# A fourth staging place for late operands, and filter groups of 1024 columns instead of 864, in an H3 convolution woven into a feed-forward network

## The chip, the cores and the metric

The kernel runs on one core of one Trainium2 chip. The metric is the device time of one execution in microseconds (us). A core has five engines with an instruction queue each: TensorE (PE in the profile, with its weight loads as PEld), VectorE (DVE), ScalarE (ACT), GpSimd (POOL) and SyncE (SP), which here does nothing but issue DMAs.

## The reference

All inputs are float32, with S = 2048 rows, D = 576 channels and a hidden width of 4608. Cut to what matters:

```python
xn = layernorm(x)                                   # x: (1, 2048, 576)
k_shift = sum(k_pad[:, t:t+S] * shift_k[:, 3-t] for t in range(4))
kv = k_shift * v
y  = irfft(rfft(kv, 2*S) * rfft(ssm_k, 2*S))[:S]    # causal long convolution, per channel
y  = y + kv * ssm_D
h  = maximum(xn @ w1, 0)                            # (2048, 4608)
out = x + xn * y + h @ w2
```

## The kernel before, in words

Two computations share the core. The feed-forward network (FFN) is nearly all of the matrix work. The hidden layer is cut into groups of columns, called quads, and each quad goes through two halves of the rows. Its matmuls are float32 products made of three products of split operands (high times high, high times low, low times high), so every operand is stored as two parts: a rounded copy, and what the copy lacks. All of them have line L575 in the profile. `psh` are the PSUM banks of the hidden layer, `hh` and `ll` its two parts after relu, `pso` the PSUM tile of an output unit of 128 rows. VectorE adds each finished output unit to an accumulator (L772). Around the first products stand small steps that combine PSUM banks: among them the ScalarE copy `psh` to `psh` (L661) and VectorE's addition to `p` (L704), for which the next products on TensorE wait.

The convolution is a second program, the generator `conv`, whose stages are fed into the FFN's instruction stream. `tick` is called after each small batch of FFN matmuls. It adds the batch's columns to one clock and a share of them to another, and when the convolution's clock says so it takes the next step of `stages`. A step yields its cost, or a negative number for a pause in FFN columns, or "wide" for a step that needs an output bank of the FFN: such a step is placed between two output units, and `borrowed()` hands it the bank that the FFN used last. Steps are thus placed by counted columns and not by what has finished. Inside a step, `here()` puts the instructions of VectorE and ScalarE behind the FFN's newest ones on these engines. Every engine works in its written order, and SP's queue too.

All data of the convolution lies in one SBUF tile, `area`, of which `view(offset, shape)` cuts pieces, and the stages use the same places one after another. In order they are:

- `later_operands`: the second half of the rows is normalised, stored and read back transposed, and then the operands for the second half of the FFN are made. There are seven of them, and each has two pieces of 512 columns. For a piece, ScalarE copies the high part into a place (L473), VectorE subtracts to get the low part (L474), and SP stores both parts together to DRAM (L476, names `ops_...`). For operands whose name begins with s, VectorE forms a difference first. The place comes from `stages_o`, a ring of three: two at REST + 2048 and one at 3072. From the seventh piece on the third place is `yf["11"]`, whose operand has been stored by then. From the seventh piece on a step also issues one load of the filter (`load_filter`, L832); there are 16 of these loads, and they are the convolution's input `ssm_k` in the order of the transform.
- the filter stage: for each of 32 positions, a copy of 288 columns is taken out of `kt` by ScalarE (L943) or VectorE (L941) into the ring `copies` of four places; one place less holds `ssm_D` at first, which VectorE adds to the filter. A `group` is the first transform of 2 x KG = 864 columns taken from the copies in sequence, 32 x 288 = 9216 in all. Its two halves go to the small banks `psf` and to the borrowed output bank, called `psg` (both L785). A half is cut wherever a copy ends, since another copy needs another matrix, and each piece costs four matmuls. ScalarE (L867) and VectorE (L869) copy both halves into `z`, a single buffer, and SP stores `z` to DRAM (L910, name `zk`), two stores for each copy that the group touches. The copies out of PSUM of the next group wait until these stores have landed. The matrices come from DRAM by `load_mat` (L838) through a ring of four, each of them used by two positions.
- the input stage: the taps and gates of k and v, and groups of 2 x CW = 1024 columns through the same `group`; then the products of the spectra, and the way back. The change does not touch them, apart from where their places in `area` begin.

The code that runs ahead of all this begins with a tile of zeros, `warm`, on which TensorE does 22 matmuls, and with the first loads.

The lines that set the two sizes and the ring's places are these:

```python
KG = 432
Z, KSO, WT = REST, REST + 4 * CW, REST + 4 * CW + 4 * NH
AREA = WT + 4 * U * P
starts = list(range(0, flat, 2 * KG))
```

Of the kernel before, what the change touches and what calls it, by code (L numbers as in the profile page):

```python
# [10 lines left out]
F32 = mybir.dt.float32  # L11
# [6 lines left out]
P = 128  # L18
# [4 lines left out]
T = S // P  # L23
NH = D // 2
# [29 lines left out]

CW = 512
NCH = NG * D // CW
KG = 432
KD = 36
KT_GAP = 6000
N_FB, N_FS, N_FK, N_FX, N_FM, N_FO = 23, 14, A2, T * (2 * KS + 1) + 2, NCH // 2, T  # L60
# [5 lines left out]
KT = 0  # L66
ROWS = 2 * KS + 8
REST = ROWS * D
Z, KSO, WT = REST, REST + 4 * CW, REST + 4 * CW + 4 * NH
AREA = WT + 4 * U * P  # L70

OPERANDS = ("00", "01", "s2", "s3", "11", "s1", "s4")
# [27 lines left out]
def h3_ffn_kernel(ctx: ExitStack, tc, x, k, v, shift_k, ssm_k, ssm_D, w1, w2, fwd, inv, mid, out):  # L100
# [300 lines left out]
    def later_operands(view, views, load_filter):  # L401


        first = HB * BT
        rows = {}
        for t in range(first, T, 2):
            rows[t] = view((t - first) // 2 * 2 * D, 2, D)
            move(rows[t], x, slice(t, t + 2))
        yield -PAUSE
        for t0 in range(first, T, 4):  # L410
            for t in range(t0, t0 + 4):
                with here():
                    stats(t, rows[t - t % 2][:, t % 2, :])
                yield W_FB / 2
            shift = xp.tile([P, 4], F32, tag="shift", name=f"shift{t0}", bufs=2)
            with here():
                inv_std(t0, 4)
                nc.vector.scalar_tensor_tensor(shift, mv[:, t0:t0 + 4, 0], -1.0, rstd[:, t0:t0 + 4],
                                               op0=OP.mult, op1=OP.mult)
            yield W_FB / 2  # L420
            for t in range(t0, t0 + 4):
                pair = rows[t - t % 2]
                with here():
                    nc.scalar.activation(pair[:, t % 2, :], pair[:, t % 2, :], AF.Identity,
                                         scale=rstd[:, t:t + 1], bias=shift[:, t - t0:t - t0 + 1])
                yield W_FB / 2
                if t % 2:
                    nc.sync.dma_start(rows_n[t // BT - HB, t % BT // 2].rearrange("t p d -> p t d"),
                                      pair)
        order = [(b, c) for b in range(HB) for c in range(5)]  # L430
        yf = {f"{b}{k}": view(HB * BT * D + (2 * b + k) * 1024, 2, 512)
              for b in range(HB) for k in range(2)}
        for n, o in enumerate(("s1", "s2")):
            yf[o] = view(REST + 1024 * n, 2, 512)
        ws = {}

        def load(n):
            if n < len(order):
                b, c = order[n]
                src = rows_n[b].rearrange("h t (g p) d -> p (h t g) d", p=32)  # L440
                w = ws[n] = view(n % 4 * 512, 512)
                for i in range(4 if c < 4 else 2):
                    d = c * P + 32 * i
                    nc.sync.dma_start(w[32 * i:32 * i + 32].rearrange("p (g d) -> p g d", d=32),
                                      src[:, :, d:d + 32])

        for n in range(2):
            load(n)
        yield -PAUSE
        for n, (b, c) in enumerate(order):  # L450
            load(n + 2)
            with here():
                if c < 4:
                    nc.vector.transpose(yf[f"{b}{c // 2}"][:, c % 2, :], ws[n])
                else:
                    v, r = (view(2048 + (2 * b + k) * 512, 512) for k in range(2))
                    nc.vector.transpose(v[:64], ws[n][:64])
                    split_rest(r.bitcast(F32R), v)
                    nc.sync.dma_start(hl_n[b], r)
            yield W_FB  # L460
        n = 0
        stages_o = Ring(*views(REST + 2048, 2, 2, 512), view(3072, 2, 512))
        for o in ("00", "11", "s1", "s2", "01", "s3", "s4"):
            for c in range(2):
                with here():
                    combine(None, yf, (o,), c)
                if o[0] == "s":
                    yield W_FB / 2
                if n == HB * 3:
                    stages_o.views = (*stages_o.views[:2], yf["11"])  # L470
                dst = stages_o.put(n)
                with here():
                    nc.scalar.activation(dst[:, 0].bitcast(F32R), yf[o][:, c, :], AF.Copy)  # L473
                    nc.vector.tensor_tensor(dst[:, 1].bitcast(F32R), yf[o][:, c, :],  # L474
                                            dst[:, 0].bitcast(F32R), OP.subtract)
                nc.sync.dma_start(ops_n[o][:, :, c, :], dst)  # L476
                if n >= 6:
                    load_filter()
                n += 1
                yield W_FS  # L480
# [340 lines left out]
    def stages(view, views):  # L821
# [15 lines left out]
        def load_mat(key, t, queue=nc.gpsimd):  # L837
            queue.dma_start(mats.put(key), fwd[t])  # L838
# [48 lines left out]
            yield -KT_GAP  # L887
        for t in range(2):
            load_mat(("k", t), t, nc.sync)
        copies = Ring(*views(KSO, 4, NH))  # L890
        skip = copies.put("skip")
        for h in range(2):
            nc.sync.dma_start(skip[h * A1:h * A1 + 1, :], ssm_D[None, h * NH:(h + 1) * NH])
# [43 lines left out]
        for e, t2 in enumerate(order):  # L937
            to = copies.put(e)
            with here():
                if e % 2:  # L940
                    nc.vector.tensor_copy(to, kt[:, :, t2])  # L941
                else:
                    nc.scalar.activation(to, kt[:, :, t2], AF.Copy)  # L943
            if e == A2 - 1:
                load(0)
            yield W_FK / 2
            while starts and min(starts[0] + 2 * KG, flat) <= e * NH + (e == A2 - 1) * NH:
                yield "wide"
                filter_group(starts.pop(0))
                yield W_FK / 2 / (len(range(0, flat, 2 * KG)) / A2)  # L950
            if e % U and e // U + 2 < T:
                load_mat(("k", e // U + 2), e // U + 2, nc.sync)


        stage["seeded"] = (3, 4)
# [285 lines left out]
                clock["conv"] -= c  # L1241
                steps -= 1

    warm = const.tile([P, 512], mybir.dt.bfloat16, name="warm")
    nc.vector.memset(warm, 0.0)
    for t in range(0, BT, 2):
        load_acc(t, queues=(nc.sync, nc.scalar))
    load_w1(0)
    load_acc(BT)
    load_acc(BT + 2)  # L1250
    for j in range(FT):
        load_w2(0, j)
    table = const.tile([P, 1], F32, name="table")
    nc.vector.memset(table, 1.0)
    nc.scalar.activation(table, table, AF.Sqrt)
    idle = [ps_h.tile([P, 512], F32, tag=f"h{i}", name=f"psw{i}") for i in range(2)]

    def keep_warm(n):
        for i in range(n):
            last = nc.tensor.matmul(idle[0], warm[:, :P], warm, start=True, stop=True)  # L1260
        return last

    done["pe"] = keep_warm(N_WARM)
    with tc.tile_pool(name="fa", bufs=1) as fa:
        block_xT(fa, 0, ("00", "01"), (None, None), block_rows(fa, 0))
        xn = block_rows(fa, 1)
        classical(0, 0, 0, 1)
        classical(0, 0, 1, 2)
        block_xT(fa, 1, ("10", "11"), ("s4", None), xn)
        load_w1(1)  # L1270
        with tc.issue_after(done["low"].ins):
            inv_std(0, 2 * BT)
        with tc.issue_after(done["centred"].ins):
            for j in range(FT):
                split_w2(0, j)
                load_w2(1, j)
        classical(0, 1, 0, 0)
        split_a(1)
        classical(0, 1, 1, 0)
        split_r(1)  # L1280
        split_b(1)
        split_d(1)
        load_w1(2)
        spread_scales(fa)

        def unit(g, b, i, upto):
            mm2(g, b, i)
            post(1, upto)

        for g in range(1, PLAIN):  # L1290
            now = "00" if g < PLAIN - 1 else "10"
            for f in range(FT):
                for i in range(2):
                    unit(g - 1, 0, 2 * f + i, "00")
                if g == f == 1:
                    posts["at"] = second_half_of_start(fa)
                classical(g, 0, f, 0, 3, now if f else "00")
            for j in range(FT):
                split_w2(g, j)
                load_w2(g + 1, j)  # L1300
            for i in range(BT):
                unit(g - 1, 1, i, now)
            classical(g, 1, 0, 0, 3, now)
            split_a(g + 1)
            if g + 1 == PLAIN:
                sums(g + 1)
            split_r(g + 1)
            classical(g, 1, 1, 0, 3, None if g == PLAIN - 1 else now)
            split_b(g + 1)
            split_d(g + 1)  # L1310
            load_w1(g + 2)
        quad(PLAIN, [(PLAIN - 1, b, i) for b in range(2) for i in range(BT)])
        post(99)
# [35 lines left out]
```

## Time and profile before

| what | value |
|---|---|
| median of 3 runs | 1017.88 us (1017.45 to 1019.43) |
| the profiled execution | 1021.45 us, of which its span 1019.7 us |
| granted TensorE clock | 1.000 |
| TensorE busy | 1004.9 us, 99% of the span |
| VectorE, ScalarE, GpSimd busy | 697.7, 436.8 and 460.5 us |
| copies (L473) that stage the second half's operands | 161.6 to 217.6 us into the span |
| filter stage, first copy to last store issued | 256 to 338 us into the span |

How to read the rows that follow. A row of the timeline begins with the start in us from the span's beginning and the duration, then engine, line, operation, what is written and what is read, and in brackets how long the engine had been idle and which event released it. A row of the waits has the engine and line that waited, what it waited for, the total, the number of times and the longest. A row of the chain has a start, a duration and the work. In a row of DMA landings the three numbers are the shortest, median and longest time from issue to landing.

### The profile page before, as it was taken

The page shows a single profiled execution, that of the slowest core. Times are in us where ns is not written, and L with a number is a line of the kernel's source. Part 1 is how long each engine was busy: PE and PEld are TensorE (multiplying, and loading weights), DVE is VectorE, ACT ScalarE, POOL GpSimd, SP SyncE. Part 2 cuts the span into 40 slices and gives each one's busy share as a digit, 9 for nine tenths or more (in the row PEclk, how much of TensorE's full clock was granted, in tenths as well). Part 3 has the DMA queues.
Part 4 walks back from the last instruction along what each step waited for, and adds up shares of the span by engine and source line. Part 5 has one row for each costly group of instructions (what it writes and reads, how often), then busy time and mean ns, then how long its engine had stood idle before and what let it go on. Part 6 is the DMA issues. An engine that isn't in the chain of part 4 may idle for free.

```text
span 1019.7 us, 17381 instructions
## 1 busy us (share of the span) xinstructions
PE 1004.9 (99%) x6502; PEld 844.4 (83%) x6502; DVE 697.7 (68%) x1059; ACT 436.8 (43%) x765; POOL 460.5 (45%) x500
## 2 busy tenths in 40 slices
PE   9999999999999999999999999999999999999997
PEld 5998999889877898898889889887777777777787
DVE  6787677774665697787768768556667666666764
ACT  7244443443455244445354444544554544532220
POOL 4335444444443855645555454424533234434450
PEclk9999999999999999999999999999999999999999
DMA  6214389898465724359862433468889879878964
GB/s 172 90 50 113 102 186 193 186 224 137 135 204 183 214 76 129 93 167 376 255 193 89 136 107 91 153 184 241 247 242 262 269 230 276 222 220 240 277 183 116
DMA packets 129720, 185.22 MB, mean 182 GB/s; under 512 B 69042, under 2 KB 83508, under 8 KB 128740
## 3 DMA queue, kind: packets, MB, share of 16 engines
q1 hardware_dynamic: 113332, 130.82, 46.2%
q0 software_dynamic: 15952, 52.40, 17.4%
q8 instruction: 51, 0.84, 0.4%
q10 hardware_dynamic: 352, 0.89, 0.3%
q14 instruction: 33, 0.27, 0.1%
HBM read 119.57 MB, written 45.62 MB: 162 GB/s over the span
## 4 chain that ended last, share of the span: by engine, by line
PE 90%; DMA 4%; DVE 3%; issue 1%; ACT 1%; POOL 1%; SPq 0%; DVEq 0%; POOLq 0%; ACTq 0%
PE pso L575 42%; PE psh L575 34%; PE psg L785 5%; PE psf L785 4%; PE psh_c L575 3%; DMA ops_s<-area 1%; DMA r<-in_w 1%; DMA zk<-area 1%; PE psw L1260 1%; DVE ll L602 1%; DVE sums L531 0%; DVE x L297 0%; PE psx L235 0%; SPq L910 0%; POOL wd L519 0%
## 5 line engine op out<-in xcount | busy, mean ns | idle before, releaser
L575 PE MATMUL pso<-w,hh 128*128 128x288 f32 x2304 | 466.8, 296 | 1.0 <-DVE area L869 0.8
L575 PEld LDWEIGHTS pso<-w,hh 128*128 128x128 f32 x2304 | 378.0, 188 | 30.8 <-issue 7.6
L575 PE MATMUL pso<-w,ll 128*128 128x288 f32 x1152 | 339.5, 295 | 0.0
L772 DVE TENSOR_TENSOR acc<-pso,acc 128x576 f32<-128x576 f32 x240 | 180.4, 754 | 123.9 <-PE pso L575 123.3
L575 PEld LDWEIGHTS pso<-w,ll 128*128 128x128 f32 x1152 | 216.2, 188 | 0.0
L519 POOL TENSOR_TENSOR wb<-sums,wb 128x512 fp32r<-128x512 f32 x33 | 47.6, 1441 | 291.8 <-ACT wb L518 266.2
L519 POOL TENSOR_TENSOR w<-r,w 128x576 fp32r<-128x576 f32 x72 | 108.1, 1509 | 124.6 <-ACT w L518 124.4
L575 PE MATMUL psh<-x,wa 128*128 128x512 f32 x396 | 102.4, 394 | 3.3 <-DVE p L704 2.2
L575 PE MATMUL psh<-xs,wb 128*128 128x512 f32 x396 | 102.1, 393 | 0.0
L575 PEld LDWEIGHTS psh<-x,wa 128*128 128x128 f32 x396 | 72.4, 188 | 18.8 <-DVE p L704 2.7
L575 PE MATMUL psh<-hl,wr 128*128 128x512 f32 x264 | 85.3, 404 | 0.8 <-ACT psh L699 0.8
L602 DVE SCALAR_TENSOR_TENSOR ll<-psh,hh 128x512 fp32r<-128x512 f32 x66 | 45.3, 687 | 55.1 <-ACT hh L597 55.1
L519 POOL TENSOR_TENSOR wa<-r,wa 128x512 fp32r<-128x512 f32 x36 | 56.5, 1570 | 54.0 <-ACT wa L518 53.9
L575 PEld LDWEIGHTS psh<-xs,wb 128*128 128x128 f32 x396 | 70.8, 188 | 11.4
L699 ACT ACTIVATE psh<-psh 128x512 f32<-128x512 f32 x33 | 19.2, 582 | 117.4 <-DVE u L697 117.4
L785 PE MATMUL psg<-area 64*64 64x512 f32 (+10 forms) x632 | 64.2, 472 | 1.5 <-issue 1.5
L575 PEld LDWEIGHTS psh<-hl,wr 128*128 128x128 f32 x264 | 45.9, 188 | 21.6 <-issue 10.8
L597 ACT ACTIVATE hh<-psh 128x512 fp32r<-128x512 f32 x66 | 39.3, 595 | 47.6 <-PE psh L575 47.4
L597 ACT ACTIVATE hh<-p 128x512 fp32r<-128x512 f32 x33 | 20.9, 634 | 88.1 <-PE pso L575 43.4
L697 DVE TENSOR_TENSOR u<-psh,u 128x512 f32<-128x512 f32 x33 | 22.8, 691 | 45.3 <-PE psh L575 45.2
L785 PE MATMUL psf<-area 64*64 64x512 f32 (+10 forms) x528 | 51.1, 451 | 0.7 <-DVE area L941 0.7
L575 PE MATMUL psh<-xs,wc 128*128 128x512 f32 x198 | 51.2, 393 | 0.0
(137 smaller groups left out, 1498.9 us busy)
## 6 DMA issues: line engine op xcount, KB each, us to landing
r<-in_w POOLq DMA_DIRECT2D x70, 288.0 KB, 4.0
area<-area SPq DMA_DIRECT2D x144, 128.0 KB, 4.8
r<-in_w POOLq DMA_DIRECT2D x35, 512.0 KB, 4.9
zk<-area SPq DMA_DIRECT2D x64, 144.0 KB, 2.9
area<-zk SPq DMA_DIRECT2D x18, 512.0 KB, 4.3
area<-zx SPq DMA_DIRECT2D x18, 512.0 KB, 6.2
zy<-area SPq DMA_DIRECT2D x18, 512.0 KB, 3.1
area<-zy SPq DMA_DIRECT2D x32, 288.0 KB, 7.2
```

The lines of the kernel that those rows point to most:

```text
L519: nc.gpsimd.tensor_tensor(w[:, 1, :n], src, w[:, 0, :n], OP.subtract)
L575: last = nc.tensor.matmul(ps, a, m, start=start and n == 0, stop=n == len(seq) - 1, skip_group_check=True)
L597: done["act"] = nc.scalar.activation(hh, ps, AF.Relu)
L602: done["ll"] = nc.vector.scalar_tensor_tensor(ll, ps, 0.0, hh, op0=OP.max, op1=OP.subtract)
L697: nc.vector.tensor_tensor(u2, x, u2, OP.add)
L699: nc.scalar.activation(x, y, AF.Copy, scale=-1.0)
L772: done["acc"] = nc.vector.tensor_tensor(two(acc[t]), ps[:, :, :NH], two(acc[t]), OP.add)
L785: done["pe"] = nc.tensor.matmul(ps, a, m, start=start, stop=stop, skip_group_check=True)
L1260: last = nc.tensor.matmul(idle[0], warm[:, :P], warm, start=True, stop=True)
```

## The change

Four things are edited.

- KG grows from 432 to 512, so that a filter group has 1024 columns and nine groups cover the 9216 columns instead of eleven. A half of 512 columns now touches two or three copies of 288.
- `copies` has six places instead of four, since a group now reaches over up to five copies. `area` grows from 13440 to 14016 columns for this. The matrix for the pair of positions after next is loaded one step later, since a group that starts later still reads the old one.
- `stages_o` is a list of 14 places, one for each piece. Pieces 0 to 5 have three places as before. From piece 6 on there are four: the two at REST + 2048, `yf["11"]`, and `yf["s1"]`, which is free by then. So a place is written again after four pieces and not after three.
- The start-up code stands inside the pool "fa", which takes `warm` as well. Its instructions are the same in the same order. The pool is closed after the first quads, and `area` may then use its space.

Lines behind L471 have numbers lower by one in the changed kernel.

```diff
-KG = 432
+KG = 512
...
-Z, KSO, WT = REST, REST + 4 * CW, REST + 4 * CW + 4 * NH
+Z, KSO, WT = REST, REST + 4 * CW, REST + 4 * CW + 6 * NH
...
-        stages_o = Ring(*views(REST + 2048, 2, 2, 512), view(3072, 2, 512))
+        two_o = views(REST + 2048, 2, 2, 512)
+        stages_o = [*two_o, view(3072, 2, 512)] * 2 + [*two_o, yf["11"], yf["s1"]] * 2
         for o in ("00", "11", "s1", "s2", "01", "s3", "s4"):
             for c in range(2):
...
-                if n == HB * 3:
-                    stages_o.views = (*stages_o.views[:2], yf["11"])
-                dst = stages_o.put(n)
+                dst = stages_o[n]
...
-        copies = Ring(*views(KSO, 4, NH))
+        copies = Ring(*views(KSO, 6, NH))
...
-            if e % U and e // U + 2 < T:
-                load_mat(("k", e // U + 2), e // U + 2, nc.sync)
+            if e % U and 2 <= e // U + 1 < T:
+                load_mat(("k", e // U + 1), e // U + 1, nc.sync)
...
-    warm = const.tile([P, 512], mybir.dt.bfloat16, name="warm")
...
     with tc.tile_pool(name="fa", bufs=1) as fa:
+        warm = fa.tile([P, 512], mybir.dt.bfloat16, name="warm")
...
```

A tile scheduler puts the DMA issues of SP where it expects them to be ready, so SP's order moves with the places. SP's queue before, from the fourth operand on (`area` is the tile of the convolution, `ops_` the stored operands, `in_` the inputs):

```order
L476 DMA ops_s2_96<-area_1166 256x1x512
L832 DMA area_1166<-in_ssm_k 64x36x32 x2
L476 DMA ops_s2_96<-area_1166 256x1x512
L476 DMA ops_01_95<-area_1166 256x1x512 x2
L476 DMA ops_s3_97<-area_1166 256x1x512 x2
L832 DMA area_1166<-in_ssm_k 64x36x32 x2
L476 DMA ops_s4_100<-area_1166 256x1x512
L832 DMA area_1166<-in_ssm_k 64x36x32 x4
L476 DMA ops_s4_100<-area_1166 256x1x512
L832 DMA area_1166<-in_ssm_k 64x36x32 x2
L893 DMA area_1166<-in_ssm_D 1x288 x2
L838 DMA area_1166<-in_fwd 128x256 x4
```

And the same stretch of SP's queue in the changed kernel:

```order
L475 DMA ops_s2_96<-area_1166 256x1x512
L831 DMA area_1166<-in_ssm_k 64x36x32 x2
L475 DMA ops_s2_96<-area_1166 256x1x512
L475 DMA ops_01_95<-area_1166 256x1x512 x2
L475 DMA ops_s3_97<-area_1166 256x1x512 x2
L892 DMA area_1166<-in_ssm_D 1x288 x2
L837 DMA area_1166<-in_fwd 128x256 x2
L475 DMA ops_s4_100<-area_1166 256x1x512
L831 DMA area_1166<-in_ssm_k 64x36x32 x3
L475 DMA ops_s4_100<-area_1166 256x1x512
L831 DMA area_1166<-in_ssm_k 64x36x32 x5
```

The stores up to the sixth operand's (s3) stand in the same order. The loads of ssm_D and two of the matrices have moved ahead of the stores of s4, and filter loads have moved behind them; two more matrix loads now stand far earlier in the queue, ahead of the second half's rows.

On TensorE the groups move. Before, the third group (counted from the first) stood behind the last product of a hidden half (`psh` from `hl` and `wr`) and ahead of an output unit's first matmuls:

```order
L575 MATMUL psh_2_2698<-hl_948,wr_2664 128x512 x2
L785 MATMUL psf<-area 64x288 x4
L785 MATMUL psf<-area 64x144 x4
L785 MATMUL psg<-area 64x144 x4
L785 MATMUL psg<-area 64x288 x4
L575 MATMUL pso_7_2935<-w_2533,hh_1_0_2692 128x288 x2
```

In the changed kernel the same place on TensorE has no group:

```order
L574 MATMUL pso_6_2937<-w_2599,hh_1_1_2655 128x288 x2
L574 MATMUL pso_6_2937<-w_2599,ll_1_1_2656 128x288
L574 MATMUL psh_2_2698<-hl_948,wr_2664 128x512 x2
L574 MATMUL pso_7_2952<-w_2533,hh_1_0_2692 128x288 x2
L574 MATMUL pso_7_2952<-w_2533,ll_1_0_2693 128x288
```

The last group of the filter stage is at the end of the copies in both. Before, on TensorE, it had 576 columns in three pieces:

```order
L575 MATMUL psh_2_3450<-xs_699,wb_3377 128x512 x6
L785 MATMUL psf<-area 64x288 x4
L785 MATMUL psf<-area 64x144 x4
L785 MATMUL psg<-area 64x144 x4
L575 MATMUL pso_3_3535<-w_3161,hh_0_0_3140 128x288 x2
```

In the changed kernel it is a full group on TensorE, in five pieces:

```order
L574 MATMUL psh_2_3446<-xs_699,wb_3369 128x512 x6
L784 MATMUL psf<-area 64x160 x4
L784 MATMUL psf<-area 64x288 x4
L784 MATMUL psf<-area 64x64 x4
L784 MATMUL psg<-area 64x224 x4
L784 MATMUL psg<-area 64x288 x4
L574 MATMUL pso_3_3545<-w_3169,hh_0_0_3148 128x288 x2
```

Both stand in front of the same output unit.

More of the change, by code (lines that the diff above doesn't have):

```diff
@@ L1242, in tick, with keep_warm @@
                 steps -= 1
-    warm = const.tile([P, 512], mybir.dt.bfloat16, name="warm")
[L1245 to L1263, printed above, removed]
-    with tc.tile_pool(name="fa", bufs=1) as fa:
+    with tc.tile_pool(name="fa", bufs=1) as fa:
+        warm = fa.tile([P, 512], mybir.dt.bfloat16, name="warm")
+        nc.vector.memset(warm, 0.0)
+        for t in range(0, BT, 2):
+            load_acc(t, queues=(nc.sync, nc.scalar))
+        load_w1(0)
+        load_acc(BT)
+        load_acc(BT + 2)
+        for j in range(FT):
+            load_w2(0, j)
+        table = const.tile([P, 1], F32, name="table")
+        nc.vector.memset(table, 1.0)
+        nc.scalar.activation(table, table, AF.Sqrt)
+        idle = [ps_h.tile([P, 512], F32, tag=f"h{i}", name=f"psw{i}") for i in range(2)]
+        def keep_warm(n):
+            for i in range(n):
+                last = nc.tensor.matmul(idle[0], warm[:, :P], warm, start=True, stop=True)
+            return last
+        done["pe"] = keep_warm(N_WARM)
         block_xT(fa, 0, ("00", "01"), (None, None), block_rows(fa, 0))
```

## The prediction

> **What bounds the kernel now.** I read the page first, then TensorE's waits, then the timeline and the chain of waits around each wait. The page:
>
> ```profile
> span 1019.7 us, 17381 instructions
> PE 1004.9 (99%) x6502; PEld 844.4 (83%) x6502; DVE 697.7 (68%) x1059; ACT 436.8 (43%) x765; POOL 460.5 (45%) x500
> ```
>
> TensorE is busy for 1004.9 of 1019.7 us. A change can shorten this kernel in two ways only: less work on TensorE, or fewer of the 15 us in which it stands still. TensorE's waits say where it stood:
>
> ```profile
> PE psh L575 <- DVE p L704: 2.2, 1, 2.2
> PE psh L575 <- ACT psh L661: 1.0, 1, 1.0
> PE pso L575 <- DVE area L869: 0.8, 1, 0.8
> PE psf L785 <- DVE area L941: 0.7, 1, 0.7
> ```
>
> Four waits lie where the change works: the first two while the second half's operands are staged, the last two at the end of the filter stage. The timeline around the first two:
>
> ```profile
> 199.01 0.69 DVE L602 SCALAR_TENSOR_TENSOR ll<-u,hh 128x512 fp32r<-128x512 f32 x1 [0.19 <-ACT hh L597]
> 201.63 0.63 ACT L473 ACTIVATE area<-area 128x512 fp32r<-128x512 f32 x1 [2.66 <-DMA ops_s<-area]
> 202.30 0.69 DVE L474 TENSOR_TENSOR area<-area 128x512 fp32r<-128x512 f32 x1 [2.60 <-ACT area L473]
> 204.18 0.68 DVE L704 TENSOR_TENSOR p<-psh,p 128x512 f32<-128x512 f32 x1
> 204.91 1.65 PE L575 MATMUL psh<-x,wa 128*128 128x512 f32 x6 [2.23 <-DVE p L704]
> 207.64 0.63 ACT L473 ACTIVATE area<-area 128x512 fp32r<-128x512 f32 x1 [0.92 <-DMA ops_s<-area]
> 209.18 0.62 ACT L473 ACTIVATE area<-area 128x512 fp32r<-128x512 f32 x1
> 210.13 0.58 ACT L661 ACTIVATE psh<-psh 128x512 f32<-128x512 f32 x1 [0.33 <-DVE ll L602]
> 210.77 1.65 PE L575 MATMUL psh<-x,wa 128*128 128x512 f32 x6 [1.01 <-ACT psh L661]
> ```
>
> The ACT copy at 201.63 is piece 9 (counted from 0). It waits 2.66 us for a store to land, because its place still holds piece 6. VectorE's subtraction waits behind it, L704 behind that, and TensorE behind L704. The copies at 207.64 and 209.18 are pieces 10 and 11; ACT works in order, so L661, for which TensorE waits next, stands behind both. The chain of waits shows the two stores, pieces 6 and 7:
>
> ```profile
> 193.76 7.79 DMA ops_s<-area
> 201.60 5.96 DMA ops_s<-area
> ```
>
> They landed at 201.55 and 207.56.
>
> **The change part by part. Staging.** From piece 6 on a place is used again after four pieces instead of three. Piece 9 takes the free place of s1 and waits for nothing. ACT was free at 201.63 - 2.66 = 198.97 and VectorE at 199.01 + 0.69 = 199.70, where the subtraction can now start, against 202.30. L704 came 204.18 - 202.30 = 1.88 us after it, so it runs from 201.58 to 202.26. TensorE began to wait at 204.91 - 2.23 = 202.68, so the 2.23 us go.
>
> Piece 10 now waits for piece 6, landed at 201.55. ACT reaches it at 207.64 - 0.92 - 2.66 = 204.06: no wait. Piece 11 follows 209.18 - 207.64 = 1.54 us later, at 205.60, and now waits for piece 7 instead of piece 8. This is the wait that the change adds. SP's queue up to piece 7 is in the same order, so I keep 207.56. Behind piece 11 on ACT stands L661: 207.56 + 0.63 + 0.58 and some 0.08 between them give 208.85, against 210.77. TensorE would have been ready at 210.77 - 1.01 - 2.23 = 207.53, so it waits 1.3 us there. **Staging gains 210.77 - 208.85 = 1.9 us** of the 3.2. The bound is how long the store of piece 7 takes; all staging stores took:
>
> ```profile
> DMA to landing us min/median/max: 5.5/6.1/7.8
> ```
>
> At 5.5 us the gain is 2.4, at 7.8 it is 0.1. I take this store's own 5.96. Pieces 12 and 13 wait for the stores of 8 and 9, which are issued before 205 and were waited for by nothing at 213 and 217. SP now stands behind the landing of pieces 10 and 11 for the ssm_D and fwd loads before it issues the last filter loads; it stood as long before, for another place, and nothing reads the filter until the first copy of it some 12 us after its loads have landed. I cost that at nothing; without that cover each us late would be a us.
>
> **Groups.** Eleven groups (ten of 864 columns, one of 576) become nine of 1024. The chain of waits gives a group of 864, and what the FFN matmuls behind it took with a group ahead and without one:
>
> ```profile
> 264.37 0.89 PE psf L785 x16
> 265.26 0.73 PE psg L785 x16
> 265.99 1.80 PE pso L575 x12
> 269.17 1.58 PE pso L575 x12
> ```
>
> 0.89 + 0.73 + 0.22 = 1.84 us each. Groups of 1024 columns stand in the input stage, one in many pieces and one in few:
>
> ```profile
> 430.64 1.02 PE psf L785 x16
> 431.66 0.86 PE psg L785 x16
> 528.71 1.02 PE psf L785 x8
> 529.73 0.86 PE psg L785 x8
> ```
>
> That is 1.88 + 0.22 = 2.10 us, with 32 matmuls or with 16. The last group, and the one ahead of it:
>
> ```profile
> 325.86 0.96 PE L785 MATMUL psf<-area 64*64 64x288 f32 x16
> 331.12 0.71 PE L785 MATMUL psf<-area 64*64 64x288 f32 x8
> 332.54 0.47 PE L785 MATMUL psf<-area 64*64 64x144 f32 x8 [0.71 <-DVE area L941]
> 333.19 0.53 PE L575 MATMUL pso<-w,hh 128*128 128x288 f32 x2
> ```
>
> Without its wait the last one took 333.19 - 331.12 - 0.71 = 1.36, and 0.22. Before: 10 x 1.84 + 1.58 = 20.0; after: 9 x 2.10 = 18.9. **Fewer groups gain 1.1 us.** Columns at the 288 boundaries now make 48 pieces instead of 43, down to 32 columns. If each matmul had a price, a half in three pieces (24 matmuls) would take at most 24 x 0.73/16 = 1.10 us by the 864 row, 0.08 over 1.02 and 0.24 over 0.86; six first and six second halves have three pieces, so at most 1.9 us. I take 0, since 16 and 32 matmuls cost the same. [...]
>
> **The z buffer.** A group's results wait in one buffer until their stores land; the next group's copies out of PSUM wait for that, and the FFN's next use of the borrowed banks waits for the copies. Stores become 80 instead of 64. SP's pace, and a group's first store:
>
> ```profile
> 279.46 0.89 PE psf L785 x16
> 281.38 1.17 SPq L910 DMA_DIRECT2D zk<-area  x2
> 283.27 2.47 SPq L910 DMA_DIRECT2D zk<-area  x4
> ```
>
> So the first store is 2.0 us behind the group, and one follows each 0.62 us. Two gaps between groups stay short, 331.12 - 325.86 = 5.26, now 5.5 with the larger group (the fourth to the fifth, and the eighth to the ninth; before there were four such). Both follow a group with ten stores: the last is issued 2.0 + 9 x 0.62 = 7.6 after its group, 2.1 after the next one's start S. Stores land after
>
> ```profile
> DMA to landing us min/median/max: 2.2/2.9/5.7
> ```
>
> and VectorE's last copy takes 0.7 (0.61 for 432 columns), so the bank is free at S + 5.0 to S + 8.5. It is needed 1.88 us (the group) and 3.24 us (333.19 to 336.43, where the wait below began) after S, at S + 5.1:
>
> ```profile
> 336.37 0.61 DVE L869 COPY area<-psf 128x432 f32<-128x432 f32 x1 [3.88 <-DMA zk<-area]
> 337.24 0.54 PE L575 MATMUL pso<-w,hh 128*128 128x288 f32 x2 [0.81 <-DVE area L869]
> 332.31 3.87 DMA zk<-area
> ```
>
> The waits are thus 0 to 3.4 us each. I take the median 2.9 for the fifth group (0.6 us) and 3.3, between it and the 3.87 above, for the ninth (1.0). The 0.7 behind L941 came from stores that landed late: that copy stands behind VectorE's copies of the eighth group, which wait for the seventh group's stores. There are now eight of these, 8.5 us ahead; at the median the last lands 2.0 + 7 x 0.62 + 2.9 = 9.2 after its group, 0.7 after the eighth starts, when nothing asks for it yet. It goes, or stays where landings are long. 1.6 after, 1.5 before: **0.1 lost**; from -1.5 to 6.8 + 0.7 - 1.5 = +6.0.
>
> **The fwd loads**, one step later, must land between one group and the next in four cases. These gaps are at least
>
> ```profile
> 284.26 0.89 PE psf L785 x16
> 292.52 0.89 PE psf L785 x16
> ```
>
> 8.3, now 8.5 us, and the piece is in the group's second half: 6.6 + 1.0 us, against a longest landing of 6.6 us among these loads.
>
> ```profile
> DMA to landing us min/median/max: 2.3/4.3/6.6
> ```
>
> Cost 0; uncovered, about a us. Moving the warm tile changes no order: 0.
>
> **Sum:** -1.9 - 1.1 + 0.1 = -2.9 us. The profiled execution took 1021.45 us (span 1019.7 and 1.75 around it) and would take 1018.55. The unprofiled runs' median lies 3.57 below it, so I predict 1015.0.
>
> **The rivals.** *The z buffer decides (slower).* If the last stores of the fourth and eighth groups take 5.7 us, the two waits are 3.4 each and L941's stays: 6.0 lost, -1.9 - 1.1 + 6.0 = +3.0 in sum, 1020.9 us. It decides from about 5.2 us on, where the two waits of 2.9 each and the 0.7 make the sum +2.0. For it: DVE waited 3.88 us for such a store at the very place, and there are now ten instead of six. Against it: the median is 2.9 and four short gaps have become two. [...]
>
> *The staging wait only moves.* If piece 7 lands as late as 7.8 us, piece 11 gives back all but 0.1: -0.1 - 1.1 + 0.1 = -1.1, 1016.8 us. For it: DMA is what binds there; against it: its own row says 5.96.
>
> *Small pieces have a price*, the bound above: -2.9 + 1.9 = -1.0, 1016.9 us.
>
> *Both waits vanish:* store at 5.5, landings at 2.2: -2.4 - 1.1 - 1.5 = -5.0, 1012.9 us.
>
> *The change doesn't do what it says:* the order shows the same staging steps with other places, so I leave it no chance.
>
> **How the numbers follow.** Forecast 0.52 (its own range 1013.5 to 1016.3), z buffer 0.11, wait moves 0.13, pieces 0.08, both vanish 0.12, elsewhere 0.04. A measurement here can tell some 0.2%, 2.0 us: below 1015.8 or above 1019.9. Faster: 0.42 of the forecast and 0.12, 0.54. Slower: 0.11 and 0.02, 0.13. Same: 0.33. The range 1012.3 to 1018.5 holds all but the z buffer's case and half of elsewhere.
>
> **What would show it.** In the profile after: no wait of ACT at piece 9 and none of TensorE behind L704; one of about 2 us at piece 11 and one of about 1.3 us of TensorE behind the copy that was L661; groups of 1.88 us; TensorE waiting about 1 us behind the ninth group and less behind the fifth. I am wrong if TensorE waits over 3 us in the filter stage, if a group takes over 2 us, or if the wait at piece 11 reaches 3 us.

## The result, and the profile after

The changed kernel is slower: 1024.3 us (median of 6 runs, 1022.56 to 1026.51) against 1019.03 (6 runs beside them and before), a ratio of 1.0056 with a 95% interval of 1.0039 to 1.0072. By the ratio that is 5.7 us more (the two medians are 5.3 apart), where 2.9 less was forecast. Its profiled execution took 1024.46 us. That is close to its median, while the profiled execution of before, 1021.45, was above all six of these runs. So the two traces are only 3.0 us of span apart, and below I account for these 3.0, which is about half of the loss.

From the page of the changed kernel:

```profile
span 1022.7 us, 17462 instructions
PE 1007.3 (98%) x6542; PEld 848.4 (83%) x6542; DVE 693.9 (68%) x1055; ACT 437.1 (43%) x761; POOL 458.6 (45%) x500
```

TensorE is busy for 2.4 us more than before, although it makes two groups fewer. The row of the granted clock shows why; it is the fourteenth of the 40 slices that is lower. Before:

```profile
PEclk9999999999999999999999999999999999999999
```

After:

```profile
PEclk9999999999999899999999999999999999999999
```

TensorE's waits, with the two that belong to the change:

```profile
PE pso L574 <- DVE area L868: 5.0, 2, 4.1
PE psh L574 <- ACT psh L660: 1.2, 1, 1.2
```

The second is the staging, and it is what was forecast. In the timeline there, ACT and TensorE:

```profile
199.06 0.62 ACT L472 ACTIVATE area<-area 128x512 fp32r<-128x512 f32 x1
...
201.68 0.68 DVE L703 TENSOR_TENSOR p<-psh,p 128x512 f32<-128x512 f32 x1
...
207.83 0.63 ACT L472 ACTIVATE area<-area 128x512 fp32r<-128x512 f32 x1 [2.09 <-DMA ops_s<-area]
208.37 0.58 ACT L660 ACTIVATE psh<-psh 128x512 f32<-128x512 f32 x1
...
209.00 1.65 PE L574 MATMUL psh<-x,wa 128*128 128x512 f32 x6 [1.22 <-ACT psh L660]
```

The copy at 199.06 is piece 9 and waits for nothing; piece 11 at 207.83 waits 2.09 us, and TensorE 1.22.

The other wait stands behind the ninth group. TensorE's timeline:

```profile
323.69 1.16 PE L784 MATMUL psf<-area 64*64 64x32 f32 x24
324.67 1.05 PE L784 MATMUL psg<-area 64*64 64x96 f32 x24
325.65 0.74 PE L574 MATMUL psh<-hl,wr 128*128 128x512 f32 x2
...
329.29 1.10 PE L784 MATMUL psf<-area 64*64 64x160 f32 x24
...
332.89 1.55 PE L574 MATMUL psh<-xs,wc 128*128 128x512 f32 x6
338.52 0.85 PE L574 MATMUL pso<-w,hh 128*128 128x288 f32 x2 [4.08 <-DVE area L868]
...
341.57 2.77 PE L574 MATMUL psh<-xs,wb 128*128 128x512 f32 x6
344.13 0.72 PE L574 MATMUL psh<-hl,wr 128*128 128x512 f32 x2
```

After a wait of 4.08 us the same six matmuls take 2.77 us instead of 1.55. The stretches of TensorE's clock (columns: length, PE busy with its count, granted clock, DMA share, GB/s):

```profile
334.04:337.46 3.42, 0.40 (x2) 1.00 0.90 260
337.46:340.87 3.41, 2.35 (x10) 0.50 1.05 361
340.87:344.29 3.42, 3.42 (x11) 0.50 1.04 358
344.29:347.70 3.41, 3.41 (x22) 1.00 1.08 323
```

For 6.83 us the clock was at half, and TensorE worked for 2.35 + 3.42 = 5.77 of them. From the granted clock of 0.50 I estimate that this work takes half as long at full clock (the six matmuls above took 1.8 times as long), so 2.9 us were lost there, beside the wait.

The chain of waits shows what the group waited for:

```profile
331.75 0.60 SPq L909
332.35 0.04 issue
332.40 5.26 DMA zk<-area
...
337.77 0.70 DVE area L868
```

It is the eighth group's tenth store. It was issued at 332.40, 3.1 us after the ninth group began, and landed 5.26 us later, although it holds 128 columns and a full one 288. Of the four stores that SP issued from 329.2 to 331.2 the trace has the landing of two, and these took less than half the time:

```profile
DMA to landing us min/median/max: 2.2/2.2/2.2
```

What came between is in GpSimd's timeline:

```profile
330.52 1.41 POOL L518 TENSOR_TENSOR w<-r,w 128x576 fp32r<-128x576 f32 x1
331.88 0.56 POOL L922 DMA_DIRECT2D area<-in_shift_k  x1
332.43 1.05 POOL L167 DMA_DIRECT2D area<-in_k  x2
333.47 1.04 POOL L167 DMA_DIRECT2D area<-in_v  x2
334.50 0.57 POOL L510 DMA_DIRECT2D r<-in_w  x1
```

The rows from 331.88 to 333.47 are the first loads of the input stage. They go into the places of the filter, so they must wait for the last copy (L940) out of it, but that had ended at 329.42. What they stood behind is the first row, the last of three additions for the weights on GpSimd, which ended at 331.93. Before, they also came right behind the third addition, but later against the groups, and the store for which the last group waited, issued at 332.31, was 2.6 us ahead of them:

```profile
333.59 1.42 POOL L519 TENSOR_TENSOR w<-r,w 128x576 fp32r<-128x576 f32 x1
334.95 0.56 POOL L923 DMA_DIRECT2D area<-in_shift_k  x1
```

What the groups themselves cost on TensorE (L785 before, L784 after, from 255 to 336 us), first before and then after:

```profile
255.00:336.00 81.00, 18.37 (x344) 1.00 0.55 174
```

```profile
255.00:336.00 81.00, 17.90 (x384) 1.00 0.55 171
```

With two changes of 0.22 us fewer, the larger groups save 18.37 - 17.90 + 0.44 = 0.9 us. The account between the two traces: staging 1.22 - 3.24 = -2.0; groups -0.9; waits for the z buffer and behind it, 4.08 and 0.88 against 0.81 and 0.71, +3.4; half clock +2.9; waits outside the change (1.2 and 0.5 against 1.5 and 0.8) -0.6. The sum is +2.8, of 3.0.

### The profile page after: what moved, and what is told of

It is laid out like the page before. It is cut to its first block, busy times and chain, and to the rows that moved or that the text cites. A ratio compares the mean times of both kernels' runs of the same rounds, so it can differ in the third digit from the quotient of the medians.

```text
span 1022.7 us, 17462 instructions
## 1 busy us (share of the span) xinstructions
PE 1007.3 (98%) x6542; PEld 848.4 (83%) x6542; DVE 693.9 (68%) x1055; ACT 437.1 (43%) x761; POOL 458.6 (45%) x500
## 4 chain that ended last, share of the span: by engine, by line
PE 89%; DVE 3%; DMA 3%; issue 2%; ACT 1%; POOL 1%; SPq 1%; ACTq 0%; POOLq 0%; DVEq 0%
PE pso L574 41%; PE psh L574 34%; PE psg L784 5%; PE psf L784 4%; PE psh_c L574 3%; DMA r<-in_w 1%; PE psw L1260 1%; DMA zk<-area 1%; DMA ops_s<-area 1%; SPq L909 1%; DVE sums L530 1%; DVE area L473 0%; DVE acc L771 0%; DVE x L297 0%; PE psx L235 0%
## 5 line engine op out<-in xcount | busy, mean ns | idle before, releaser
L784 PE MATMUL psg<-area 64*64 64x512 f32 (+13 forms) x656 | 64.2, 463 | 1.2 <-issue 1.2
L574 PE MATMUL psh<-x,wc 128*128 128x512 f32 x198 | 51.2, 394 | 0.0
```

The lines of the kernel that those rows point to most:

```text
L574: last = nc.tensor.matmul(ps, a, m, start=start and n == 0, stop=n == len(seq) - 1, skip_group_check=True)
L784: done["pe"] = nc.tensor.matmul(ps, a, m, start=start, stop=stop, skip_group_check=True)
```

## The experiments

My theory after the result (A): the staging is a gain as forecast, and the whole loss stands behind the ninth group, in three steps. Ten stores instead of six from one queue are issued later; the last of them meets GpSimd's loads and lands late; TensorE then stands still so long that its clock falls. The rivals: the staging costs (B), the many small pieces or the groups themselves cost, or the clock falls for another reason (C), and the stores are late by themselves, without the loads (D). Ratios are to the kernel before, run on the same chip, with their 95% intervals; 0.001 is 1.0 us. A difference between two of these ratios is uncertain by about 2 us, and each trace is one execution.

**Each part alone.** The first experiment is the kernel before with only this edit:

```diff
-        stages_o = Ring(*views(REST + 2048, 2, 2, 512), view(3072, 2, 512))
+        two_o = views(REST + 2048, 2, 2, 512)
+        stages_o = [*two_o, view(3072, 2, 512)] * 2 + [*two_o, yf["11"], yf["s1"]] * 2
```

> The kernel before with the fourth staging place alone (groups of 864 columns, four copies, as before). Theory A (the loss is the ninth filter group's wait, the staging is a gain): the two waits of 2.23 and 1.01 us become one of about 1.2, as in the changed kernel's trace, so about 2.0 us less than before, 1017.0 against 1019.0. Theory B (a new wait at the eleventh piece eats the gain, or the other order on SP delays the filter loads): no gain or a loss, 1019 or more.

Measured 1017.31 us, ratio 0.9987 (0.9978 to 0.9995): 1.3 us less. In its trace what is left of the staging waits is this row:

```profile
PE psh L574 <- ACT psh L660: 1.0, 1, 1.0
```

Theory B falls. The counterpart is the changed kernel with the old three places:

```diff
-        stages_o = [*two_o, view(3072, 2, 512)] * 2 + [*two_o, yf["11"], yf["s1"]] * 2
+        stages_o = Ring(*views(REST + 2048, 2, 2, 512), view(3072, 2, 512))
```

> The changed kernel with the old three staging places; nine groups of 1024 columns and all else as changed. Theory A: the ninth group's wait of about 4 us and the slower clock behind it stay, if GpSimd's loads still meet the last stores of the eighth group: 7 us over before, 1026. If their meeting depends on how early the staging lets everything run, the wait is shorter and the time lies between 1019 and 1022. Theory B (staging is what costs): about 1018, 1.1 us under before.

1023.73 us, ratio 1.0053 (1.0038 to 1.0069). The loss is in the groups, and it does not need the earlier staging. The two parts alone add up to 5.4 - 1.3 = 4.1 us, the whole change to 5.7, which the intervals don't tell apart. The row behind the ninth group:

```profile
338.92 0.53 PE L575 MATMUL pso<-w,hh 128*128 128x288 f32 x2 [2.53 <-DVE area L869]
```

The wait is 2.53 us in this trace, and the clock was at half for 3.41 us behind it. The wait and the time both lie between what the two forms of A expected, so this run doesn't say whether the staging adds to the ninth group's wait.

**The wait taken away.** The ninth group's results go into a part of the filter's places that is free by then (the main lines):

```diff
...
+                zs[:] = [z if len(starts) > 1 else view(11 * D, 2, 2 * CW)]
                 filter_group(starts.pop(0))
+                zs[:] = [z]
...
```

> The changed kernel, but the ninth group is copied out into a part of the area that is free by then, so that its copies don't wait for the eighth group's stores. Same order on every engine. Theory A: the wait of 4.08 us goes, and with it the half clock that cost some 2.5 us: 6.6 us less than the changed kernel, 1017.7. Theory C (the loss is in the groups themselves, in their many small pieces and 80 stores): at most the wait's 4 us go and the clock still falls, 1020 or more.

1018.71 us, ratio 0.9991 (0.9980 to 1.0002). Against the changed kernel's 1.0056 that is 6.6 us less, as A said. Of the wait for the z buffer only the fifth group's is left:

```profile
PE pso L574 <- DVE area L869: 1.2, 1, 1.2
```

So the loss is the ninth group's wait and what followed from it. The groups' pieces are not it: this kernel has all of them.

**The clock apart from the wait.** Twelve matmuls into a bank that nobody reads fill the time in which TensorE waits:

```diff
...
+                scrap = fft_psum()
+                for n in range(12):
+                    in_turn(scrap, hid[g, b, 0][0][:, :P], hid[g, b, 0][0], True, True)
...
```

> The changed kernel, with twelve matmuls of 512 columns added on TensorE just ahead of the output unit that waits for the ninth group; they write a bank that nobody reads, take some 3.1 us (0.26 each, as the FFN's) and fit in the wait of 4.1. The wait itself and all else stay. Theory A (TensorE's clock falls to half because it stands still for 4 us, and that costs 2.5 us beside the wait): the granted clock stays at 1.0 and the time falls by 2.5, to 1021.8. Theory C (the clock falls for another reason): it falls as before, and the time stays at 1024.3.

1021.62 us, ratio 1.0028 (1.0016 to 1.0039), 2.8 us less than the changed kernel. The timeline of TensorE:

```profile
332.77 1.55 PE L574 MATMUL psh<-xs,wc 128*128 128x512 f32 x6
334.15 2.88 PE L790 MATMUL psf<-hh 128*128 128x512 f32 x12
336.87 0.47 PE L574 MATMUL pso<-w,hh 128*128 128x288 f32 x2
```

The work behind runs at full clock. In this execution the ninth group's last copy ended at 336.75, about when the twelve were done, so that without them TensorE would have stood still for some 2.5 us, and not for 4.08 as in the trace of the changed kernel. The time over nine runs agrees with the 2.5 us forecast, though the two intervals just touch. The mean granted clock was 0.997 to 1.000 in these nine runs, and 0.995 to 0.998 in the six of the changed kernel. The second half of theory C falls: the clock fell because TensorE stood still.

**The loads beside the stores.** I first tried to delay them in the program, with shorter pauses behind them:

```diff
-            if e == A2 - 1:
-                load(0)
...
+        yield -12000
+        load(0)
...
-            yield -PAUSE / 4
+            yield -1000
```

> The changed kernel, but GpSimd's first loads of the input stage stand 12000 FFN columns (some 5 us) later, and the pauses behind them are shorter by as much, so that all groups keep their places. The z buffer is waited for as in the changed kernel. Theory A (the eighth group's last two stores land 5 us instead of 2.2 after issue because these loads fill the DMA engines): they land after 2.2, TensorE waits about 1.6 us instead of 4.1, the clock stays at 1.0, and the time is 5 us less than the changed kernel, 1019.3. Theory D (ten stores on one queue are late by themselves, whatever runs beside them): the wait stays near 4 us and the time at 1024.

1022.8 us, ratio 1.0042 (1.0028 to 1.0057). This run tells nothing about the loads, because they did not move: they came 2.6 us after the ninth group's start, as in the changed kernel, right behind the third addition. GpSimd's queue has nothing else at this place, so its next instruction is the same:

```profile
331.44 0.56 POOL L922 DMA_DIRECT2D area<-in_shift_k  x1
```

The wait was 3.30 us. What held these loads back was GpSimd's work ahead of them, and not their place in the program. So I put them into SP's queue, behind the ten stores:

```diff
-                nc.gpsimd.dma_start(sk[:, -t, :], shift_k[-t:1 - t, :].to_broadcast([P, D]))
+                nc.sync.dma_start(sk[:, -t, :], shift_k[-t:1 - t, :].to_broadcast([P, D]))
...
-            queues = (nc.sync if t > 1 else nc.gpsimd,) * 2
+            queues = (nc.sync,) * 2
...
```

> The changed kernel, but the first loads of the input stage (shift_k, and k and v of the first positions) go through SP's queue, which has them behind the eighth group's ten stores, instead of GpSimd's, where they were issued beside the last two of these. A later delay of these loads in the program had not moved them on GpSimd's queue, so this is the test of theory A that the run with later loads was meant to be. Theory A (the loads lengthen the landing of the last two stores from 2.2 us to about 5): the last store, issued at about 332.4, lands at 334.6, TensorE waits 1.5 us instead of 4.1 and keeps its clock: 5 us less than the changed kernel, 1019.3. Theory D (the stores are late by themselves): the wait stays near 4 us, 1024.

1020.98 us, ratio 1.0022 (1.0009 to 1.0035), 3.4 us less than the changed kernel of the 5 expected. The tenth store in the chain of waits:

```profile
332.81 3.55 DMA zk<-area
```

It took 3.55 us instead of 5.26, and TensorE waited 1.87 instead of 4.08. Of these 2.2 us, 1.7 are the landing; the other 0.5 are the issue, which came 2.6 us after the group's start instead of 3.1. The landing did not come down to 2.2: GpSimd's next transfers, a weight load (L510) and a matrix, moved up to 332.80 in place of the others. That fits A, by which the landing follows what is loaded beside the store, but no run here has that store with nothing beside it. D in its strict form falls. The clock still fell in this execution, behind a wait of 1.87 us:

```profile
334.81:338.22 3.41, 1.54 (x10) 1.00 0.96 256
338.22:341.63 3.41, 3.41 (x13) 0.50 1.03 287
```

**The pace of one queue.** Five of the eighth group's stores go through ScalarE's queue:

```diff
...
-                    nc.sync.dma_start(at_t(zk, order[e])[:, :, r * NH + c:r * NH + c + w],
+                    queue = nc.scalar if r and len(starts) == 1 else nc.sync
+                    queue.dma_start(at_t(zk, order[e])[:, :, r * NH + c:r * NH + c + w],
...
```

> The changed kernel, but five of the eighth group's ten stores (those of the second half of the channels) are issued from ScalarE's queue instead of SP's. Theory A: SP issues its fifth store some 3 us earlier, at about 329.2, all ten land before GpSimd's loads begin at 331.9, the ninth group's copies don't wait, and the clock stays: 6.6 us less than the changed kernel, 1017.7, plus what the issues hold up on ScalarE (at most 5 x 0.6 us, if each delayed TensorE). Theory D (the wait is for DMA bandwidth, not for SP's pace): the last store lands no earlier, 1024.

1019.41 us, ratio 1.0012 (1.0000 to 1.0024): 4.5 us less, where 6.6 were expected. All ten stores were issued by 1.2 us after the ninth group's start, and the copies out of that group's banks waited for none of them. But the loads moved too: ScalarE, which now issues stores, reached its copies of the weights later, GpSimd's additions stand behind those, and the loads began 4.3 us after the group's start instead of 2.6. So the run doesn't price the pace apart from the loads. The group itself stood still for 0.4 us, for its last copy:

```profile
PE psg L784 <- DVE area L941: 0.4, 1, 0.4
```

The 2.1 us that are missing are not settled. Part of them is at the fifth group, on which this edit has no hold:

```profile
302.46 0.74 PE L574 MATMUL pso<-w,hh 128*128 128x288 f32 x2 [2.76 <-DVE area L868]
```

Its wait was 0.88 us in the changed kernel's trace and 2.76 here, with 3.41 us of half clock. The fourth group has ten stores too, and weight loads are issued 1.1 us behind the last of them, whose own issue took 1.60 us here. But this trace is of the slowest of the twelve runs, and the nine runs with a mean clock of 0.999 or 1.000 have a median of 1019.3 too, so the clock can't be all. What the five issues hold up on ScalarE, priced at up to 3 us ahead of the run, was not measured.

**Better versions.** With the ninth group in its free place, I added a fifth staging place (some lines left out):

```diff
-        stages_o = [*two_o, view(3072, 2, 512)] * 2 + [*two_o, yf["11"], yf["s1"]] * 2
+        stages_o = [*two_o, view(3072, 2, 512)] * 2 + [*two_o, yf["11"], yf["s1"], view(3520, 2, 512)] * 2
...
-                if n >= 6:
+                if n >= 8:
                     load_filter()
...
```

> The changed kernel with the ninth group copied into a free part of the area, and with a fifth staging place from the seventh piece on (the first filter loads are issued two pieces later for that). Theory A: beside the 6.6 us of the ninth group, the wait of 2.1 us at the twelfth piece goes and with it TensorE's 1.2: 1016.5, 2.7 us under before. If the later filter loads hold up the filter stage, 1018 or more.

1016.79 us by the median, but a ratio of 0.9991 (0.9979 to 1.0003): no gain that can be told from the kernel before, nor from the kernel with the free place alone, whose ratio was the same. The staging wait is gone from the trace; the fifth group's is there with 1.0 us. So I took that one as well:

```diff
+                    queue = nc.scalar if r and len(starts) == 5 else nc.sync
...
```

> The kernel of the run before with five staging places and the ninth group in a free place, and with five of the fourth group's ten stores issued from ScalarE's queue. Five of that kernel's twelve runs had a mean clock of 0.997 or 0.998 and took 1018.5 to 1020.9, the other seven took 1015.5 to 1016.8. Theory A: the fifth group's wait (0.9 to 2.8 us in the traces so far) is what lowers the clock in those five; with its stores done some 3 us earlier nearly all runs fall in the lower band, median 1016.0, 2.4 us under before. Theory D: the wait depends on the DMA engines alone, the split stays, median 1016.8 or more.

1016.8 us, ratio 0.9982 (0.9973 to 0.9991). One of eleven runs took over 1018 us with a mean clock of 0.997, where it had been five of twelve. That fits A but is too few to show it, and no trace has one of those five. The one slower run of the eleven is the profiled one; its clock fell behind a wait of 2.17 us at 901, outside the change. No z wait is left in its trace, but at the fifth group TensorE now stands still for a copy into `copies`:

```profile
PE psg L784 <- DVE area L943: 1.3, 1, 1.3
```

The wait of 1.0 us has thus only changed its place in this trace. The median did not reach the 1016.0, and is the 1016.8 of theory D. The last kernel has the staging places and the free place for its last group, but the old groups of 864 columns, with their four copies:

```diff
-KG = 512
+KG = 432
...
```

> The kernel before (eleven groups of 864 and 576 columns) with the fourth and a fifth staging place, and with the last group copied into a free place. Theory A: the fourth place alone gave 1017.3; the fifth takes away TensorE's 1.0 us behind the twelfth piece, the last group's place takes what is left of its wait (0.2 us in that trace): 1016.2, 2.2 to 3 us under before, with no wait over 1.5 us in the stages of the change and so a clock at 1.0. If groups of 1024 columns are worth their 1.1 us once their waits are gone, this kernel is that much above the best with 1024.

1016.6 us, ratio 0.9979 (0.9969 to 0.9989): 2.1 us less than before and 7.8 less than the changed kernel, the fastest of all in ratio. TensorE's longest waits in its trace:

```profile
PE psw L1263 <- DVE table L1257: 1.2, 1, 1.2
PE psh L574 <- ACT psh L698: 0.9, 2, 0.6
```

None of them is in the stages of the change. The two best kernels cannot be told apart, so the 0.9 us that larger groups save did not show in any time; the wait of 1.3 us above, if the other runs had it too, is more than that.

## Why the prediction was wrong, point by point

- **Staging: right.** 1.9 us forecast, 2.0 between the traces, 1.3 (0.5 to 2.2) with this part alone. L703 started at 201.68 (forecast 201.58), the new wait at piece 11 was 2.09 us (about 2), TensorE's 1.22 (1.3).
- **Fewer groups: right.** 1.1 forecast, 0.9 measured. A group with 48 matmul records takes 325.65 - 323.69 = 1.96 us, one with 32 in the input stage 1.88: 0.08 for 16 records at most, so 0.2 us for the 40 that were added.
- **The z buffer, ninth group: this step failed.** The sum had the z buffer at 0.1 us lost; it cost 3.4 us of waits and 2.9 of clock. The step said that the bank is free from S + 5.0 to S + 8.5, S being the start of the group, and took a wait of 1.0. It was free at 338.46, S + 9.2, outside my bounds, and the wait was 4.08. Of the 3.1 us that the term was short, 1.0 are the issue and 2.0 the landing. The last store was issued 3.1 us after S and not 2.1, as one issue of SP, the second, took 1.65 us and the others came 0.64 apart; the same issue took 1.0 to 1.3 us in the traces of the runs with the groups alone and with the free place, and why is open. And the store landed after 5.26 us, where I took 3.3, between two rows of before.
- **The landing was the mistake of method.** I took one distribution for all stores (2.2, 2.9, 5.7) and its median, as if chance chose. The trace of before had the pattern. The store that took 5.70 there, issued at 323.89, stood behind these loads:

```profile
322.04 0.78 POOL L500 DMA_DIRECT2D r<-in_w  x1
322.81 1.05 POOL L503 DMA_DIRECT2D r<-in_w  x2
323.85 0.57 POOL L838 DMA_DIRECT2D area<-in_fwd  x1
```

The stores of the ninth group's wait landed in 2.2 us ahead of GpSimd's loads and in 3.5 to 5.3 beside them. This is not the whole of it: the 3.87 us at 332.31, on which the prediction leaned, had no load of GpSimd issued within 2.6 us of it, and what held that store is open. I should have asked which loads stand beside the last store after the change. They could be placed: the loads of the input stage stand behind GpSimd's three additions, and these behind ScalarE's copies of the weights. Before, ScalarE came late to them, because it waited for a store in the group ahead:

```profile
328.59 0.53 ACT L867 ACTIVATE area<-psf 128x432 f32<-128x432 f32 x1 [6.22 <-DMA zk<-area]
```

In the changed kernel that wait was gone. The loads now began at 331.88, S + 2.6, against 334.95 - 331.12 = S + 3.8 before, while the last stores moved from S + 1.8 to S + 3.1. The two crossed.
- **The clock: missing.** The prediction allowed the change two ways only, less work on TensorE or less standing still. The third is that the same work takes longer: TensorE did less and was busy for 2.4 us more. No term had that. It cost 2.9 us in the trace by the estimate above, 2.8 by the run with the filled wait.
- **The fifth group:** 0.6 forecast, 0.88 in the trace, and up to 2.76 in another kernel with the same code there. L941's 0.7 went, as forecast, and the fwd loads cost nothing, as forecast.
- **The rival "the z buffer decides"** was the nearest case. It had the right place and direction, but two waits of 3.4 us and L941's 0.7, where there were 4.08, 0.88 and none. That its 5.2 us meets the 5.26, and its +3.0 the 3.0 between the two traces, is luck: it had too many waits and no clock. Its chance of 0.11 came from the same median. The row that spoke for it, 3.87 us at the very place, was nearer evidence than a distribution from elsewhere.

## What to carry to other kernels

Before a landing time is taken from a distribution, split it by what else was being loaded at the time (here 2.2 us ahead of GpSimd's loads, 3.5 to 5.3 beside them), and then ask what the change puts beside the transfer that counts: here an earlier stage triggered earlier loads, at S + 2.6 instead of S + 3.8. A larger piece of work per buffer made more bytes leave in one burst (1024 columns in ten stores, where the group ahead of the last had 864 in six), and with one buffer the next piece waited for the last of them. Where TensorE is the bound, price a wait at its length, and ask whether it also costs the clock, as those of 1.87, 2.53, 2.76, 3.30 and 4.08 us in the filter stage did here and one of 2.23 us in the staging did not. By my estimate from the granted clock of 0.50 this came to half of 3.41 us, 1.7, behind the shorter ones and to 2.9 behind the one of 4.08.

## What the runs showed of the hardware

The granted clock was at half for 3.41 us after the waits of 1.87 us (the loads on SP's queue), 2.53 (the groups alone) and 2.76 (two queues), for some 3.4 us after the one of 3.30 (the later loads; an estimate from the mean clocks of 0.93 and 0.90 in the 10 us from 330 and from 340 us), and for 6.83 us after the one of 4.08. The trace with the wait of 2.17 us has a mean clock of 0.997, as have those with one such fall. The trace of the groups alone has 0.997 too, with the fall behind its 2.53 us, so its other wait of 1.7 us shows none. Before, no fall followed the wait of 2.23 us from 202.68 to 204.91 (columns as above):

```profile
200.15:203.56 3.41, 2.53 (x14) 1.00 1.34 191
203.56:206.97 3.41, 2.06 (x11) 1.00 1.25 275
206.97:210.40 3.43, 2.78 (x21) 1.00 0.60 230
```

So the length of a wait did not decide alone: one of 1.87 us cost the clock and one of 2.23 us did not. What else decided was not shown.

Stores were issued earlier when ScalarE's queue took half of them: the last one 1.2 us after the group's start instead of 3.1. Beside GpSimd's loads the last store landed late: in 5.26 us, and in 3.55 with the first of these loads moved behind the stores, where two stores issued ahead of the loads took 2.2.
